# Means of v copied by engines instead of transfers, and a new order of the opening, in an attention and gated-MLP kernel

## The chip, the cores and the metric

One core of one Trainium2 chip. The metric is the device time of one execution in microseconds (us); the median of three runs is 638.13 us (636.65 to 638.30).

## The reference

```python
# q, k, v: (4, 8, 768, 64); w_in: (512, 2048); w_out: (2048, 512)
k_sum = k.reshape(B, H, 24, 32, D).max(axis=3)
v_sum = v.reshape(B, H, 24, 32, D).mean(axis=3)
scores_l = scale * q @ k^T            # kept where |i - j| < 16
scores_s = scale * q @ k_sum^T + log(32)
a = softmax(concatenate([scores_l masked, scores_s]))
attn = a @ concatenate([v, v_sum])
x = attn as (3072 tokens, 512)
h = x @ w_in
out = (h * cos(h)) @ w_out
```

Each query sees 31 neighbours and 24 summaries of its head: block maxima of k, block means of v.

## The kernel before

The 3072 tokens are eight blocks of 384 (two for each batch entry). A block has four attention groups, `a` to `d`, of two heads each (`Group`, so `c1` is the third pair of heads of block 1). Then come steps (`Step`, `s0` to `s127`), one for a block and a slice of 128 of the 2048 hidden columns: 12 `up` products (L728, or in four chunks L740), the gate on ScalarE and VectorE, and 9 `down` products (L788). Products are made of a high and a low part of each operand. Steps `s0` to `s5` are block 0 with slices 0 to 5, `s6` to `s21` are block 1 with all 16 slices, `s22` to `s31` are block 0 with the rest.

A weight slice (`Slice`, `w0` to `w15`) is loaded by SP (L391, L395; 1 MB), taken apart by ScalarE (`ab` L403, `sh` L409), joined by VectorE (`fb` L416) and split into a high part (`hi`, L370 on ScalarE or L372 on VectorE) and a low part (`lo`, L376 on VectorE or GpSimd).

An attention group of the first two blocks goes: loads of q, k, v by SP (L454, L475, L483); transposes on PE (`tk`, `tq`) and copies (`ck`, `cq`, `ks`); mask and score products (`ms` L556, `sc` L581) into two PSUM banks; minimum (`mx` L599, VectorE); six exponentials (`ex` L616, ScalarE); reciprocal (`iv`); `normalize` (`nm` L632, GpSimd); transposes of the probabilities (`tp` L641) and copies (`cp`); `values` (`va` L685, PE) into one bank; high and low part of x (`xh`, `xl`). For `values`, the tile `vn` of a group has 120 partitions: 96 rows of v, loaded by `v`, and 24 block means, brought by `m` (`load_vs`).

The means of batch entry 0 come from 24 products over v (`vm`, L911), read out of PSUM by ScalarE (`ve`, two copies) to `all_means`, a part of the tile `early`. For the eight groups of blocks 0 and 1, `load_vs` then brings 128 columns of them to each of six rows of `vn`, on partitions 96 to 119. For later batch entries it loads from other summaries (`v1_0` and on: `l` loads, `s` sums).

The order of everything is written by hand in `ORDER`, one word for each operation (`group.operation.arguments`; the last letter is the engine: `a` ScalarE, `v` VectorE, `p` GpSimd; digits are PSUM banks or rooms). Every engine and every issuing queue works off its own part of it in that order, and each of them waits in place when an instruction isn't ready. `h0` to `h7` are products of the identity with itself that nothing reads.

Of the kernel before, what the change touches and what calls it, by code (L numbers as in the profile page):

```python
# [1038 lines left out]
```

## Time and profile before

| | |
|---|---|
| median of 3 runs | 638.13 us (636.65 to 638.30) |
| span of the profiled execution | 636.0 us |
| PE busy | 621.8 us (98%) |
| VectorE (DVE) busy | 419.0 us (66%) |
| ScalarE (ACT) busy | 323.8 us (51%) |
| GpSimd (POOL) busy | 195.1 us (31%) |
| DMA queue of SP (q1) | 72.62 MB |
| DMA queue of ScalarE (q10) | 0.72 MB |

The span reaches from the first to the last instruction of one profiled execution; the time of a run is about 2 us longer at the median. Busy shares are means over stages with different limits: what an edit in one stage is worth is read from that stage. In the chain and in the waits, "X <- Y" says that X waited for Y, as far as the semaphore events show; where Y had long been done, it was something else, often a transfer. SPq and ACTq are the queues from which SP and ScalarE issue transfers.

### The profile page before, as it was taken

How to read it: one execution, taken by the hardware profiler on the slowest of the kernel's cores; microseconds unless marked ns; L12 is line 12 of the kernel's file. 1: busy time of each engine (PE TensorE's matmuls, PEld its weight loads, DVE VectorE, ACT ScalarE, POOL GpSimd, SP SyncE). 2: the span in 40 equal slices, each digit the busy share in tenths (PEclk: the TensorE clock that was granted, in tenths of full speed). 3: DMA queues.
4: the chain of work that ended last, by engine and by line, in shares of the span. 5: the costliest groups of instructions: out<-in, count | busy, mean ns of one | idle time of the engine just before them, and what ended most of it. 6: DMA issues, size and time to landing. Idle time of an engine off the chain costs nothing.

```text
span 636.0 us, 12130 instructions
## 1 busy us (share of the span) xinstructions
PE 621.8 (98%) x4568; PEld 545.6 (86%) x4568; DVE 419.0 (66%) x814; ACT 323.8 (51%) x606; POOL 195.1 (31%) x210
## 2 busy tenths in 40 slices
...
GB/s 223 264 239 227 313 127 231 177 63 128 95 137 130 120 92 180 99 83 107 101 101 142 112 80 99 123 63 71 111 93 66 117 74 55 112 38 16 1 1 49
DMA packets 171306, 74.11 MB, mean 117 GB/s; under 512 B 136944, under 2 KB 160112, under 8 KB 171248
## 3 DMA queue, kind: packets, MB, share of 16 engines
q1 hardware_dynamic: 169856, 72.62, 45.3%
q10 hardware_dynamic: 1392, 0.72, 0.5%
q8 instruction: 36, 0.59, 0.4%
q14 instruction: 22, 0.18, 0.1%
HBM read 54.43 MB, written 16.52 MB: 112 GB/s over the span
## 4 chain that ended last, share of the span: by engine, by line
PE 90%; DVE 5%; DMA 2%; ACT 2%; ACTq 1%; issue 1%; SPq 0%; POOL 0%; DVEq 0%; POOLq 0%
PE banks L728 40%; PE banks L788 40%; PE banks L685 3%; PE banks L569 3%; DMA early<-in_v_dram 1%; PE banks L932 1%; DVE stage L416 1%; PE banks L740 1%; ACTq L490 1%; PE banks L581 1%; ACT sc L616 1%; DVE w L376 1%; PE banks L911 0%; PE banks L518 0%; DVE first L372 0%
## 5 line engine op out<-in xcount | busy, mean ns | idle before, releaser
L728 PE MATMUL banks<-xh,w 128*128 128x384 f32 x976 | 255.5, 337 | 0.5 <-DVE t L760 0.5
L788 PE MATMUL banks<-w,gh 128*128 128x512 f32 x768 | 196.5, 392 | 0.0
L728 PEld LDWEIGHTS banks<-xh,w 128*128 128x128 f32 x976 | 176.8, 188 | 3.1 <-issue 0.8
L788 PEld LDWEIGHTS banks<-w,gh 128*128 128x128 f32 x768 | 142.6, 188 | 31.1 <-DVE gh L372 1.6
L728 PE MATMUL banks<-xl,w 128*128 128x384 f32 x488 | 163.2, 334 | 0.0
L376 POOL TENSOR_TENSOR gl<-t,gh 128x384 fp32r<-128x384 f32 x63 | 65.9, 1049 | 286.8 <-DVE gh L372 152.2
L748 ACT ACTIVATE t<-banks 128x384 int32<-128x384 f32 x128 | 62.0, 489 | 126.4 <-PE banks L728 59.8
L751 DVE SCALAR_TENSOR_TENSOR t<-t,banks 128x384 f32<-128x384 int32 x128 | 69.2, 547 | 68.7 <-ACT t L748 67.9
L788 PE MATMUL banks<-w,gl 128*128 128x512 f32 x384 | 108.0, 391 | 0.0
L756 ACT ACTIVATE t<-t 128x384 f32<-128x384 f32 x128 | 65.9, 523 | 63.6 <-DVE t L751 63.3
L728 PEld LDWEIGHTS banks<-xl,w 128*128 128x128 f32 x488 | 91.6, 188 | 0.4
L760 DVE TENSOR_TENSOR t<-t,banks 128x384 f32<-128x384 f32 x128 | 69.5, 548 | 33.1 <-ACT t L756 32.1
L788 PEld LDWEIGHTS banks<-w,gl 128*128 128x128 f32 x384 | 71.6, 188 | 15.7 <-POOL gl L376 0.5
L370 ACT CAST gh<-t 128x384 fp32r<-128x384 f32 x66 | 33.6, 513 | 43.3 <-DVE t L760 24.9
L632 POOL TENSOR_TENSOR sc<-sc,r 128x720 f32<-128x720 f32 x28 | 39.0, 1392 | 47.3 <-DVE r L629 41.5
L604 POOL TENSOR_TENSOR sc<-sc,m 128x720 f32<-128x720 f32 x24 | 34.4, 1433 | 49.6 <-DVE m L596 49.6
L376 DVE TENSOR_TENSOR gl<-t,gh 128x384 fp32r<-128x384 f32 x65 | 36.5, 565 | 12.5 <-ACT gh L370 7.6
L372 DVE CAST gh<-t 128x384 fp32r<-128x384 f32 x62 | 23.1, 373 | 18.1 <-PE banks L788 14.9
L588 DVE SCALAR_TENSOR_TENSOR sc<-banks,mask 128x360 f32<-128x360 f32 x48 | 24.5, 524 | 12.6 <-PE banks L569 12.4
L622 DVE TENSOR_REDUCE r<-sc 128x6 f32<-128x726 f32 x24 | 21.6, 902 | 14.1 <-ACT sc L611 14.0
L376 POOL TENSOR_TENSOR w<-stage,w 128x1024 fp32r<-128x1024 f32 x8 | 19.7, 2468 | 33.5 <-DVE w L372 22.2
L611 ACT ACTIVATE sc<-sc 128x720 f32<-128x720 f32 x24 | 19.4, 807 | 19.0 <-POOL sc L604 18.8
(117 smaller groups left out, 611.0 us busy)
## 6 DMA issues: line engine op xcount, KB each, us to landing
...
```

What stands on the lines that cost most here:

```text
L370: eng.copy(out=out, in_=in_)
L372: eng.tensor_copy(out=out, in_=in_)
L376: eng.tensor_tensor(out=lo, in0=src, in1=hi.bitcast(F32), op=ALU.subtract)
L588: nc.vector.scalar_tensor_tensor(out=self.sc.rearrange("p (c h) n -> p c h n", h=2)[:, :, hh, :], in0=self.sp[hh], scalar=SCALE, in1=mask[ ...
L604: nc.gpsimd.tensor_tensor(out=self.sc, in0=self.sc, in1=self.m.unsqueeze(2).broadcast_to([P, U, NK]), op=ALU.subtract)
L632: nc.gpsimd.tensor_tensor(out=self.sc, in0=self.sc, in1=self.r.unsqueeze(2).broadcast_to([P, U, NK]), op=ALU.mult)
L728: nc.tensor.matmul(out=self.h, lhsT=w_of(name, self.f)[:, c * P : (c + 1) * P], rhs=x_of(self.blk, part, c), start=n == 0, stop=n == last,)
L748: nc.scalar.activation(out=self.t.bitcast(I32), in_=self.h, func=AF.Copy, scale=1.0 / TWO_PI, bias=0.25)
L751: nc.vector.scalar_tensor_tensor(out=self.t, in0=self.t.bitcast(I32), scalar=-TWO_PI, in1=self.h, op0=ALU.mult, op1=ALU.add)
L756: nc.scalar.activation(out=self.t, in_=self.t, func=AF.Sin, scale=-1.0, bias=-0.5 * math.pi)
L760: nc.vector.tensor_tensor(out=self.t, in0=self.t, in1=self.h, op=ALU.mult)
L788: nc.tensor.matmul(out=accs[self.run][i], lhsT=g[:, i * P : (i + 1) * P], rhs=w_of(name, self.f), start=self.first and n == 0, stop=self.l ...
```

## The change

`load_vs` gets an engine as its argument. For blocks 0 and 1 the engine copies the means from `all_means` to the 24 partitions of `vn`, where ScalarE issued a transfer from SBUF to SBUF. For that, `all_means` moves from partitions 0 to 23 of `early` to partitions 96 to 119, the ones to which the copies go. In the order, `c1.m` and `a0.m` are given to VectorE, `d1.m` to ScalarE, and `c0.m`, `d0.m`, `b0.m`, `a1.m` and `b1.m` to GpSimd. The first 559 of the 2098 words of `ORDER` stand in a new order, up to `s20.ga` in block 2; from there on the two are the same. They are the same operations; among them 164 have another bank, room or engine. Group b is now the first to be scored (before: a); the loads `v1_0` to `v1_3` stand behind those of most weights; slices 3, 7 and 11 have their high part on ScalarE and 4, 6, 8, 10 and 12 on VectorE (before the other way round); the low parts of slices 6, 9, 12 and 13 move to GpSimd and that of 15 to VectorE; the sums `v1_0.s` and `v1_4.s` move to GpSimd. The diff is cut: of the order only lines that stand for the beginning of both, up to the first steps.

```diff
-h0.w.3 h2.w.0 h4.w.1 a0.k a0.q b0.q a0.tk.1.5 c0.k a0.tk.0.0 a0.ms.7.6 a0.ks.1 d0.k b0.tq.3 a0.ks.0 b0.k a0.tq.4 c0.q
-a0.ck.1.a a0.ck.0.a h7.w.5 b0.cq.a a0.cq.v a0.sc c0.tk.0.0 c0.tk.1.2 b0.tk.0.4 c0.ks.0 c0.ck.0.a a0.mx.0 w1.l.6 h5.w.1
-a1.q c0.tq.0 h1.w.1 d0.q a0.ex.0 c0.ck.1.v b0.ck.0.a d0.tk.0.6 c0.ks.1 a0.iv b0.tk.1.1 b0.ks.0 d0.tk.1.2 c0.ms.3.7
-c0.cq.v b0.ms.5.0 c0.sc v0_0.l d0.ck.1.a d0.ks.1 b0.ck.1.a d0.ks.0 b0.ks.1 d0.ck.0.v b0.sc w1.ab.0 b1.q w1.sh c0.mx.1
-h6.w.2 a1.tq.6 a1.ms.1.4 v0_1.l v1_0.l d0.tq.2 a1.cq.v c0.ex.1 d0.cq.a a1.sc d0.ms.6.2 d0.sc b0.mx.2 c1.q w1.fb a0.nm
-w1.hi.v a0.tp.1.3 b0.ex.2 v0_0.vm.0 d0.mx.0 d0.ex.3 v0_1.vm a0.v a0.cp.1.a w1.lo.p c0.iv a1.mx.1 v0_1.ve.a b0.iv
-b1.tq.5 a0.tp.0.3 b1.cq.v b1.ms.2.6 b1.sc w0.l.7 d0.iv c0.nm b0.nm a0.m d0.m b0.m d1.q v1_0.s.0.v a1.ex.0 h3.w.5
-a0.cp.0.v d1.m b1.mx.2 c0.m c1.tq.3 v1_1.l c0.tp.0.5 d0.nm c0.v a1.iv a1.nm a1.m c0.tp.1.0 a0.va.4 c1.ms.7.1 c1.cq.v
-c0.cp.0.v d1.tq.3 d0.v a0.xh.a c1.sc v1_1.s.p w2.l.6 b0.v d1.cq.v a0.xl w0.ab.1 b0.tp.1.3 b0.tp.0.5 c0.cp.1.v w0.sh
-d0.tp.0.4 c0.va.0 b1.ex.1 d0.tp.1.6 v1_2.l c1.mx.0 w5.l.1 w0.fb w0.hi.v a1.v w0.lo.p d0.cp.0.a c1.ex.2 b1.iv d0.cp.1.v
-c1.m d1.ms.4.2 c0.xh.v d1.sc c0.xl d0.va.0 b1.nm d1.mx.1 b0.cp.0.a b0.cp.1.v a1.tp.0.7 w2.ab.1 c1.iv a1.tp.1.6 c1.nm
-s1.u.0.3 w2.sh d0.xh.v d1.ex.3 d0.xl b0.va.1 b0.xh.v s0.u.0.5 b0.xl v1_2.s.p s0.u.2 s1.u.2 s1.u.3 a1.cp.0.v c1.tp.1.7
-s1.u.1 s0.u.3 w2.fb w2.hi.v a1.cp.1.a d1.iv d1.v c1.v c1.tp.0.2 s0.u.1 s1.tu.0 w4.l.6 w5.ab.0 a1.va.4 s0.tu.1 w2.lo.v
-w5.sh v1_3.l s0.re d1.nm s1.re s2.u.0.6 s2.u.2 s2.u.3 c1.cp.0.a d1.tp.1.1 c1.cp.1.v c1.va.2 d1.tp.0.0 w3.l.7 s0.si
-w5.fb w5.hi.v d1.cp.1.a b1.tp.0.7 w5.lo.v s1.si s1.ga s0.ga d1.cp.0.a b1.v s2.u.1 d1.va.1 b1.tp.1.0 s5.u.0.5 a1.xh.a
-c1.xh.a w8.l.0 a1.xl s1.hi.0.a s0.hi.1.a d1.xh.v d1.xl s1.lo.0.v s0.lo.1.v w4.ab.1 b1.cp.1.a w4.sh v1_3.s.v s5.u.2
-s2.tu.0 s5.u.3 s2.re b1.m v1_4.l s5.u.1 w4.fb s0.dh.1.0.3 s2.si s0.dl s2.ga s2.hi.1.v s2.lo.1.p w3.ab.0 b1.cp.0.v
-c1.xl w4.hi.a s1.dh s1.dl s2.dh s2.dl w4.lo.v b1.va.4 w3.sh s4.u.0.6 s4.u.2 w9.l.1 b1.xh.a w3.fb w3.hi.v b1.xl s4.u.3
-w3.lo.p s4.u.1 w8.ab.1 s5.tu.1 w7.l.7 s6.up.4 v1_4.s.0.v s4.tu.0 s4.re w8.sh v1_5.l s4.si s5.re s3.u.0.2 s5.si w9.ab.0
...
+h0.w.3 h2.w.0 h4.w.1 b0.k b0.tk.0.0 b0.q h3.w.2 a0.q a0.tq.7 b0.tk.1.4 b0.ck.0.v b0.ck.1.a a0.k b0.ks.0 a0.tk.0.5
+a0.cq.a a0.ck.0.a b0.ks.1 b0.ms.6.3 c0.k c0.q a0.ks.0 b0.tq.2 d0.q b0.cq.v a0.tk.1.0 a0.ck.1.v a0.ks.1 a0.ms.1.4 d0.k
+b0.sc h6.w.7 d0.tq.5 b0.mx.2 c0.tq.2 w1.l.6 d0.cq.v b0.ex.2 v0_1.l a0.sc a0.mx.0 c0.cq.a d0.tk.0.0 d0.tk.1.7 h1.w.6
+d0.ks.1 c0.tk.0.6 d0.ck.0.v d0.ck.1.a a1.q d0.ms.3.5 c0.ck.0.v h5.w.2 b0.iv c1.q a0.ex.0 d0.ks.0 c0.tk.1.7 v0_0.l
+w1.ab.1 w0.l.7 c0.ks.1 c0.ck.1.v w1.sh a0.v c0.v b1.q c0.ks.0 d0.sc d0.mx.1 h7.w.0 a0.iv c0.ms.2.0 w1.fb w2.l.6 a0.nm
+d1.q d0.v b0.v c0.sc d0.ex.3 a1.tq.6 c1.tq.7 a0.tp.0.3 c0.mx.2 a1.cq.a a1.ms.4.6 w1.hi.v c0.ex.1 a0.tp.1.1 a0.cp.0.v
+a1.sc a1.mx.2 d0.iv w1.lo.p v0_0.vm.2 v0_1.vm a1.ex.0 c0.iv w5.l.1 b0.nm v0_1.ve.a c1.cq.v a0.cp.1.v c1.m.v c1.ms.7.3
+a0.m.v c0.nm c0.m.p d0.nm c1.sc w0.ab.1 c0.tp.0.1 w0.sh a1.iv a0.va.0 c0.tp.1.2 a0.xh.a a1.v c1.mx.0 c0.cp.0.v
+c0.cp.1.v c1.ex.2 b0.tp.0.5 c0.va.4 b1.tq.7 a0.xl c0.xh.v w0.fb d0.tp.0.0 b1.ms.1.3 b1.cq.a d0.tp.1.6 d0.m.p c1.iv
+b1.sc w0.hi.v d1.tq.7 a1.nm d0.cp.0.a c0.xl d0.cp.1.a w2.ab.0 c1.v b1.mx.0 d1.ms.0.4 w2.sh d1.cq.v b0.tp.1.2 d0.va.6
+b0.m.p b0.cp.1.v w2.fb w4.l.6 d1.sc b0.cp.0.a d0.xh.v d1.mx.2 w3.l.7 a1.tp.1.2 w0.lo.p s1.u.0.7 d1.v b1.ex.1 s1.u.2
+b0.va.5 s0.u.0.1 d0.xl d1.ex.3 b0.xh.v w5.ab.1 c1.nm w2.hi.v a1.m.p s1.u.3 b0.xl v1_0.l c1.tp.0.6 s0.u.2 w5.sh w2.lo.v
+s0.u.3 b1.v w8.l.0 a1.cp.1.a a1.tp.0.5 s2.u.0.4 s0.u.1 d1.iv s1.u.1 c1.tp.1.3 s0.tu.0 a1.cp.0.v w5.fb s0.re s0.si
+s2.u.2 s1.tu.1 a1.va.5 c1.cp.1.a w5.hi.v d1.nm c1.cp.0.a w5.lo.v s2.u.3 a1.xh.a s0.ga b1.iv s0.hi.1.a a1.xl s1.re
+d1.tp.1.0 s2.u.1 d1.tp.0.2 d1.m.a s0.lo.0.v s5.u.0.3 w9.l.1 s1.si b1.nm s5.u.2 s1.ga s5.u.3 s2.tu.0 s2.re s0.dh.6.5.1
+s2.si s0.dl s1.hi.0.v s2.ga c1.va.7 w4.ab.0 s1.dh s1.lo.1.p b1.tp.0.4 s5.u.1 c1.xh.v d1.cp.0.v s2.hi.1.v w4.sh s1.dl
+c1.xl w4.fb d1.cp.1.a s2.dh w4.hi.v s2.lo.0.p b1.m.p s5.tu.0 w3.ab.1 d1.va.7 v1_0.s.0.p w4.lo.v s4.u.0.2 b1.cp.0.v
+w3.sh s5.re s4.u.2 s5.si s4.u.3 b1.tp.1.0 v1_1.l d1.xh.v s4.u.1 w3.fb s2.dl s4.tu.1 s5.ga s5.hi.0.v b1.cp.1.a w3.hi.a
+b1.va.4 b1.xh.v w3.lo.p s4.re s5.dh b1.xl s4.si v1_1.s.p s5.lo.0.v w8.ab.1 w7.l.7 d1.xl s6.up.0 v1_2.l s3.u.0.7 s4.ga
+s4.hi.0.a s3.u.2 w8.sh s3.u.3 s3.u.1 s11.up.3 s4.lo.1.v s6.tu.1 s3.tu.0 s6.re w8.fb s6.si s3.re w8.hi.v s6.ga w9.ab.0
+s3.si s10.up.2 w8.lo.p s3.ga w9.sh s4.dl w9.fb v1_2.s.p s3.hi.1.a s4.dh s3.dh s3.lo.1.v s3.dl s11.tu.0 w10.l.2 s11.re
+s5.dl w7.ab.1 s11.si w7.sh w9.hi.a s6.hi.1.v s5.ta.1.v s11.ga s6.lo.1.p s10.tu.1 s5.ta.2.v w7.fb v1_3.l s14.up.4
...
@@ -485,11 +484,9 @@
-        def load_vs(self):
+        def load_vs(self, eng=None):
             if not self.b:
-                nc.scalar.dma_start(
-                    out=self.vn[W:NK], in_=means[self.pr].unsqueeze(1).broadcast_to([NB, U, P])
-                )
+                copy(eng, self.vn[W:NK], means[self.pr].unsqueeze(1).broadcast_to([NB, U, P]))
                 return
...
@@ -871,7 +868,7 @@
-    all_means = carve(early, 1280, NB, H * D)
+    all_means = early[W:NK, 1280 : 1280 + H * D]
     means = [all_means[:, i * P : (i + 1) * P] for i in range(NG)]
```

## Rows read from the trace of the kernel before

**Rows 1.** The profile's page: span and instructions of the profiled execution

```profile
span 636.0 us, 12130 instructions
```

**Rows 2.** Stretches: busy us (instructions) of five engines, PE clock, DMA share, GB/s

```profile
0.00:69.00 69.00, 59.73 (x779) 44.75 (x780) 50.34 (x120) 46.31 (x140) 30.63 (x56) 0.98 0.99 244
32.00:40.00 8.00, 6.68 (x113) 5.93 (x114) 5.91 (x13) 6.54 (x24) 3.75 (x6) 0.79 0.85 228
69.00:620.00 551.00, 550.48 (x3739) 491.60 (x3740) 361.91 (x681) 273.00 (x458) 162.45 (x153) 1.00 0.41 103
```

**Rows 3.** PE's waits over the run: total us, times, longest

```profile
PE banks L685 <- ACT pt L370: 2.7, 2, 2.4
PE banks L685 <- ACT sc L616: 2.1, 1, 2.1
PE banks L685 <- DVE w L372: 1.9, 1, 1.9
```

**Rows 4.** Chain that ended last, 26 to 34 us: start, us, what

```profile
27.51 1.04 ACTq L490
...
29.48 1.26 ACTq L490
```

**Rows 5.** Timeline around 45 us: start, us, engine, line, [idle before <- releaser]

```profile
44.70 0.79 ACTq L490 DMA_DIRECT2D late<-early  x1
...
45.61 0.59 ACT L370 COPY pt<-banks 120x512 f32<-120x512 f32 x1 [3.47 <-DMA early<-in_v_dram]
...
46.25 0.92 PE L685 MATMUL banks<-pt,early 120*64 120x64 f32 x24 [2.35 <-ACT pt L370]
```

**Rows 6.** Timeline, 60 to 70 us; packets of q10, 64:66 and 66:69

```profile
60.22 0.79 ACTq L490 DMA_DIRECT2D late<-early  x1
...
q10 hardware_dynamic: 113, 0.05, 11.5%
...
q10 hardware_dynamic: 43, 0.02, 3.3%
...
69.01 0.92 PE L685 MATMUL banks<-pt,late 120*64 120x64 f32 x24 [1.87 <-DVE w L372]
```

**Rows 7.** Timeline of PE, 27 to 38 us: scores, transposes

```profile
27.85 1.09 PE L581 MATMUL banks<-kd,late 64*64 64x96 f32 x48
...
30.16 0.82 PE L641 MATMUL banks<-ident,late 128*120 128x128 f32 x6
...
34.67 1.81 PE L581 MATMUL banks<-kd,qd 64*64 64x96 f32 x48
...
36.41 1.53 PE L641 MATMUL banks<-ident,sc 128*120 128x128 f32 x6
```

**Rows 8.** All DMA queues over the first 40 us

```profile
DMA packets 21578, 9.62 MB, mean 240 GB/s; under 512 B 16568, under 2 KB 21009, under 8 KB 21571
```

**Rows 9.** Groups by line to 165 us: busy us, mean ns, idle before

```profile
L372 DVE CAST w<-stage 128x1024 fp32r<-128x1024 f32 x7 | 4.8, 689 | 0.2
...
L370 ACT COPY first<-kd 128x576 f32<-128x576 f32 x4 | 2.7, 670 | 2.8 <-PE banks L569 2.8
...
L987 POOL MEMSET mask<- 128x384 f32 x1 | 0.4, 418 | 0.0
...
L376 POOL TENSOR_TENSOR w<-stage,w 128x1024 fp32r<-128x1024 f32 x8 | 19.7, 2468 | 33.5 <-DVE w L372 22.2 <-ACT w L370 10.0 <-DMA late<-in_moe_w_out_dram 1.3
...
L632 POOL TENSOR_TENSOR sc<-sc,r 128x720 f32<-128x720 f32 x6 | 8.4, 1393 | 7.8 <-DVE r L629 4.4 <-DMA x<-in_v_dram 3.4
...
L599 DVE TENSOR_REDUCE m<-banks 128x3 f32<-128x360 f32 x16 | 7.7, 524 | 0.5 <-PE banks L581 0.4
...
L372 DVE COPY pt<-banks 120x512 f32<-120x512 f32 x4 | 2.7, 684 | 0.1
```

**Rows 10.** Timeline, 51 to 54 us: GpSimd beside VectorE

```profile
51.04 1.18 DVE L376 TENSOR_TENSOR w<-stage,w 128x1024 fp32r<-128x1024 f32 x1
...
51.27 2.21 POOL L632 TENSOR_TENSOR late<-late,r 128x720 f32<-128x720 f32 x1 [2.65 <-DVE r L629]
```

More of the change, by code (lines that the diff above doesn't have):

```diff
@@ new lines @@
+s7.up.3 s5.st.1 s10.re w7.hi.a w9.lo.p s5.ta.0.a s11.hi.0.a v1_3.s.v s11.lo.0.p s10.si s6.dh.5.7.6 w10.ab.0 w6.l.6
+s6.dl v1_4.l w10.sh s10.ga s5.st.2 w7.lo.v s15.up.2 s8.up.1 s10.hi.1.a v1_4.s.0.p s10.dh a2.q w10.fb s10.lo.1.v w6.ab.1
+v1_5.l s7.tu.0 s8.tu.1 s7.re s7.si w6.sh w10.hi.v s11.dh s8.re v1_5.s.v s7.ga s8.si w6.fb w10.lo.p s7.hi.1.a s10.dl
+s7.lo.1.v s8.ga s15.tu.0 w12.l.7 s8.hi.0.v w12.ab.0 v1_6.l w13.l.6 s15.re w6.hi.v s11.dl s7.dh s8.lo.0.p w12.sh w6.lo.p
+s15.si v1_6.s.v v1_7.l w12.fb s16.up.3 s15.ga w13.ab.1 w12.hi.v s15.hi.1.v w13.sh s16.tu.1 s8.dl s15.lo.0.p w13.fb
@@ new lines @@
+s9.tu.0 w15.lo.v s19.tu.1 s13.dh w14.ab.0 s19.re b2.ks.0 s19.si s9.re w14.sh w11.lo.p s18.dh s18.dl s21.up.0 s19.ga
+w14.fb s9.si c2.kt.1 b2.q s19.hi.1.a s17.up.4 c2.kt.0 s19.lo.1.p a2.kw.a s9.ga s17.tu.1 s13.dl c2.ks.0 a2.sc.3.2 s17.re
+s19.dh w14.hi.a s9.hi.0.v s17.si a2.z.1 s19.dl b2.kw.v s17.ga s9.dh b2.qt d2.k s9.lo.1.v c2.ks.1 a2.z.0 b2.sc.4.1
+w14.lo.p a2.mx.0 s17.hi.1.v s20.up.3 b2.z.0 s23.up.2 s21.tu.0 b2.z.1 a2.su d2.kt.1 s26.up.1 s21.re s17.lo.0.v a2.ex.0
+s20.tu.1 b2.mx.0 b2.su c2.kw.a s17.dh s20.re s20.si a2.sm c2.q s21.si d2.kt.0 c2.qt a2.iv s21.ga a2.nm a2.pt.0 v2_0.l
@@ L66 @@
+c2.sc.0.4 s17.dl d2.q v2_0.s.1.p s20.ga a2.po b2.ex.1 v2_1.l b2.sm c2.z.0 s21.hi.1.a s20.hi.0.a s20.lo.0.v s23.tu.1
 b2.iv s23.re s9.dl s21.dh c2.z.1 a2.pi d2.qt s23.si s20.dl d2.ks.1 s21.lo.1.p s20.dh s21.dl d2.ks.0 s21.ta.2.0.a b2.nm
@@ new lines @@
+b3.sc.2.1 d2.pi d2.va.0 d2.xh.v d2.xl s32.up.6 s32.tu.1 s32.re s32.si s32.ga s32.hi.0.a v2_5.l v2_5.s.p s31.fe.1.0
+s31.ad.1 s33.up.0 s36.up.7 s34.up.4 s33.tu.0 s33.re b3.z.0 s32.lo.1.v s33.si s33.ga s33.hi.1.v a3.ex.0 s34.tu.1
+s31.fe.2.1 s31.ad.2 s38.up.0 b3.z.1 b3.mx.1 v2_6.l s31.st.1 s34.re a3.sm c3.kw.a s35.up.1 s34.si s34.ga s32.dh.2.4.5
+s34.hi.0.a s32.dl s33.dh s33.lo.0.p s33.dl s34.dh c3.q s31.fe.0.0 s31.ad.0 v2_6.s.p a3.v v2_7.l s34.lo.1.p s34.dl c3.qt
+s35.tu.0 s35.re s35.si s35.ga s36.tu.1 s35.hi.1.v s35.lo.0.p s35.dh s35.dl s36.re s36.si c3.sc.1.3 s31.st.0 d3.q
```

222 lines of the change are left out of this document (101 added, 121 removed).

## The prediction

> **What bounds the kernel now.** I read the page first, then busy time by stretches, then PE's waits, and last the instructions around each wait. The span is 636.0 us [rows 1] and TensorE (PE) is busy for 98% of it, so only time in which PE stands still can be won. The stretches say where that is: PE is busy for 59.73 of the first 69 us and for 550.48 of the next 551 [rows 2]. What it idles in the last 16 us is not touched: the new order meets the old one again at `s20.ga` in block 2, with the same PE work behind it. So the sum is made in the first 69 us, where PE idles for 9.3 us. What is saved there moves the end one to one, as long as the full stretch behind it stays full.
>
> PE's waits over the whole run name three of about 2 us, all at the `values` products (L685) [rows 3]; what else they name is at the very start. I went to each of the three.
>
> The first ends at 33.08 us. The chain runs from the products over v (L911) through ScalarE's copies of the means into three DMA issues of L490 (the first and the third here 1.04 and 1.26 us) [rows 4], and then through a1's six exponentials to PE. ScalarE issues those transfers itself, and the exponentials stand behind the first three in its queue; a0's `values` need the PSUM bank that they read.
>
> The second ends at 46.25 us. ScalarE, done with c1's exponentials, stands in front of the issue `c1.m` until 44.70, when the load of b0's v lands; the copy of b0's probabilities waits behind it and starts at 45.61, after 3.47 us of idle time, and PE after that, 2.35 us late [rows 5]. Nothing in that copy needs the load: the wait is the issue's own.
>
> The third ends at 69.01. The profile names a VectorE cast, which belongs to a weight slice and not to `b1.va`. What `b1.va` does need is its means: their transfer was issued at 60.22, the DMA view has no packet of ScalarE's queue from there to 64 us, and 113 and then 43 packets moved from 64 to 66 and from 66 to 69 [rows 6]. A transfer of 72 KB takes about 8 us here, because it shares the DMA engines with the weights. So all three waits belong to the eight transfers.
>
> **Part 1, the transfers go.** Removed from PE: 2.10 + 2.35 + 1.87 = 6.3 us. After the first wait the granted clock is 0.79 on average from 32 to 40 us (part of it at 1.2 GHz, the rest at 2.4), against 1.00 behind 69 us [rows 2], and the same work takes longer: a group of score products 1.81 against 1.09 us, six transposes 1.53 against 0.82 [rows 7]. That is 1.4 us, which goes with the wait that came before it. Together 7.7 us. ScalarE also gets back eight issues of 0.79 us or more [rows 4 to 6], at least 6.3 us, and the DMA engines 0.58 MB (8 x 72 KB), beside the 9.62 MB that they move in the first 40 us [rows 8]. I count neither again.
>
> **Part 2, the copies that replace them.** Each copies 24 partitions of 768 numbers. No row shows this copy; the nearest are VectorE's cast of 1024 numbers, 0.69 us, and ScalarE's copy of 576, 0.67 [rows 9]. By length that is 0.52 us on VectorE (two) and 0.9 on ScalarE (one). For GpSimd (five) the ends are its memset of 384, 0.42 us, doubled to 0.84, and its subtraction of 1024, 2.47, cut to 1.85 [rows 9]; I take 1.2, nearer the first, since a copy has one input. Two stand on PE's path: `c1.m` and `a0.m` on VectorE ahead of a0's `values`, behind ScalarE's two copies of the means. PE has c1's masks and scores and c0's first transposes meanwhile, about 2.1 us, so 0.4 us is left. The five on GpSimd stand between `normalize` operations of 1.39 us [rows 9], and the queue is far from full (30.6 of 69 us [rows 2]). At 1.85 each, b0's would come 2 us later and still before its `values`, since the probabilities are copied later yet; they cost nothing, and at most 1 us without that cover.
>
> One row speaks against using GpSimd: its `normalize` took 2.21 us instead of 1.39 while VectorE ran a weight subtraction beside it [rows 9, 10]. The Trainium skill (SBUF — State Buffer, section "Who interferes with whom") says that the two share a port pair, and that a VectorE instruction with two SBUF inputs contends with a GpSimd instruction that reads SBUF. The trace agrees with that 0.8 us. By this rule one such collision in front of `c0.va` would make the sum 0.8 us smaller.
>
> For the third wait, the Trainium skill (DMA: Bandwidth & Descriptors, section "Anatomy of one DMA — SWDGE (gpsimd) path") gives a fixed cost of about 2.0 us for a transfer, on another issue path. By it b1's means would have been there at about 62.5 us, the third wait would not be theirs, and the sum would be 1.9 us smaller. The packets of rows 6 speak against this, and I leave the sum as it is.
>
> **Part 3, the new order.** It touches 559 steps of 2098, the same ones before and after, so PE's work is the same. I added up durations of this trace along the new text, queue by queue. ScalarE is lighter by about 13 us over the stretch (issues, and casts given to VectorE and GpSimd), VectorE almost equal, GpSimd heavier by about 19. At the first `down` products VectorE has some 42 us of work behind it and ScalarE 40, against PE's 49; before it was 46 and 51 against 52. So ScalarE no longer runs level with PE. New small waits, each followed to its producer: b0's scores now come first, behind one more pair of identity products, 0.5 us; the products over v write bank 2, which c0's exponentials still read, 0.5; the means above, 0.4; `c0.va` behind c1's minima (2 x 0.52) and two copies (0.68 and a shorter one) on VectorE [rows 9], 0.9; the first chunks of slices 2 and 4 behind their low parts (1.18 [rows 10]), 0.4 + 0.3; `b1.va` behind its ScalarE copy, 0.3. The sum is 3.3 us. Bounds: 1 us, if only half of the means, the bank and `c0.va` remain, and 6 us, if each is nearly twice as long.
>
> Loads move on SP's queue. Four loads of v summaries (`v1_0` to `v1_3`) move behind the weights of the first steps, and `w0` and `w2` move ahead of most of v. DMA is nearly full up to 30 us either way. By bytes in issue order (9.6 MB in 40 us), b0's v is complete at about 37 to 41 us and its `values` stand at about 42; b1's v comes at about 57 against 64. I count nothing; without that cover it is 1 to 2 us, which is in the bounds. Farther on, the load of slice 6 moves behind a store of partial sums (`s5.st.1`), to about 83 us by my count, some 10 us later than it was. Its first use is at about 106 us, and landing and conversion take some 16 us. I put it at nothing; it is the first rival.
>
> **The sum.** 7.7 - 3.3 = 4.4 us, with bounds 7.7 - 6 = 1.7 and 7.7 - 1 = 6.7. Span: 636.0 - 4.4 = 631.6 us. The median of the runs, 638.1, is 2.1 above the profiled span, and I carry that: 633.7 us.
>
> **Rivals.** (A) The gain comes, and is partly given back between 90 and 140 us, because slices 6, 12, 13, 15, 11 and 14 arrive later against a PE that is earlier. For it: each load waits for a free place, and a store now stands among them. Against: by my count 5 us of slack at each. At 2.5 us given back the time is 636.2. (B) The change does not do what it says: the waits were really for arriving data, and PE waits as long for the loads of v and weights instead. For it: DMA is at 0.99 of its time in the first 69 us [rows 2]. Against: the second wait ended within 1 us of an issue that needs no v for the copy behind it. Time 637.5 to 638.5. (C) Slower: VectorE's queue stands still at `c1.m.v` until the means are there, and the minima of c1, b1 and d1, copies and weight joins all stand behind it. The two loads of v that feed the means now have `w1` and four loads of q among or ahead of them. I expect the second at about 26 us and the means at 31; every microsecond after that is PE's. To lose 1.9 us the means must be some 6 to 7 us late, which wants loading at about two thirds of the present rate. Against: the same bytes stood ahead of them before (5.3 MB in both orders). At 9 us late the time is 638.1 - 4.4 + 9 = 642.7.
>
> **How the numbers follow.** The forecast has 0.66, A 0.14, B 0.10, C 0.10. A measurement tells about 0.3% (1.9 us) from no change. Faster by more: nearly all of the forecast and a third of A, 0.71. Same: the rest of A, B, and a little of both neighbours, 0.18. Slower: C and its like, 0.11. The forecast's own range is 638.1 - 6.7 to 638.1 - 1.7, or 631.4 to 636.4. I widen it down to 630.8, since the idle time leaves a little more, and up to 637.3 for A and the near side of B; about 0.2 is left out.
>
> **What would show it.** Right: no DMA issues on ScalarE before the steps; PE idle below 6 us in the first 65; no wait of over 1 us at L685; clock 1.00 from 28 to 40 us; b1's `values` near 64 us; PE full from there to 620. Wrong: a wait at L685 or L740 that a v load or a weight ends (B), gaps between 90 and 140 us (A), VectorE idle until the ScalarE copies of L370 into `early` end well after 31 us (C).

## The result, and the profile after

The change makes the kernel slower: 643.2 us at the median (642.15 to 644.1) against 638.2 (636.65 to 639.27) for the kernel before beside it, a ratio of 1.008 [1.006, 1.011]. Forecast were 633.7 us, between 630.8 and 637.3. The page of the kernel after:

```profile
span 641.9 us, 12137 instructions
PE 624.2 (97%) x4568; PEld 544.9 (85%) x4568; DVE 435.3 (68%) x819; ACT 319.7 (50%) x596; POOL 217.5 (34%) x227
```

VectorE is busy 16 us longer than before (419.0), with five instructions more. Its stretches (columns as in [rows 2]):

```profile
0.00:69.00 69.00, 62.18 (x819) 46.69 (x820) 56.90 (x124) 48.06 (x141) 37.64 (x57) 1.00 0.95 233
32.00:40.00 8.00, 6.36 (x127) 5.43 (x129) 7.59 (x17) 6.38 (x19) 7.10 (x5) 1.00 0.91 227
...
69.00:90.00 21.00, 20.51 (x106) 18.30 (x104) 18.12 (x25) 16.08 (x23) 14.31 (x13) 1.00 0.53 183
90.00:115.00 25.00, 20.87 (x93) 18.14 (x94) 20.89 (x26) 13.68 (x18) 12.85 (x9) 0.93 0.62 189
115.00:165.00 50.00, 48.55 (x303) 42.49 (x302) 44.99 (x80) 32.27 (x50) 21.07 (x17) 1.00 0.57 129
165.00:620.00 455.00, 454.51 (x3173) 404.54 (x3172) 284.39 (x548) 203.16 (x353) 129.60 (x132) 1.00 0.37 92
```

The opening did gain: TensorE is busy for 62.18 us of the first 69 instead of 59.73, at the full clock where before it fell to 0.79 [rows 2]. b1's `values` start at 67.23 us instead of 69.01 [rows 6], without the wait, and 12 more `up` products of 0.17 us stand ahead of them: 1.78 + 2.1 = 3.9 us. Then it is lost. Before, PE was full from 69 us on [rows 2]; now it idles for 4.1 us between 90 and 115, with the clock at 0.93 there, and for 1.5 us between 115 and 165. From 3.9 us ahead to a span 6.0 us longer (5.98 before rounding), the kernel loses 9.9 us behind 67 us.

```profile
67.23 0.92 PE L682 MATMUL banks<-pt,late 120*64 120x64 f32 x24
```

PE's waits over the run (total, times, longest), the first in place of those of [rows 3]:

```profile
PE banks L725 <- DVE t L757: 2.7, 3, 1.9
PE banks L785 <- ACT gh L369: 2.1, 1, 2.1
PE banks L929 <- POOL ident masks.py:199: 1.4, 1, 1.4
PE banks L502 <- DMA qn<-in_q_dram: 1.0, 1, 1.0
```

The wait of 2.1 us is at 100.8 us, behind a VectorE that stood 2.3 us for a load of v; the one of 1.9 us is at 108.5. What VectorE and GpSimd do around them (start, us, what; L260, L269 and L271 belong to the sums of v, L375 on GpSimd is a low part of weights, L757 is the multiplication of the gate for which PE waits):

```profile
98.03 1.04 DVE L260 TENSOR_REDUCE part_sum<-kn 96x64 f32<-96x512 f32 x1 [2.33 <-DMA kn<-in_v_dram]
...
100.80 1.65 PE L785 MATMUL banks<-w,gh 128*128 128x512 f32 x6 [2.09 <-ACT gh L369]
...
102.75 1.02 POOL L375 TENSOR_TENSOR gl<-t,gh 128x384 fp32r<-128x384 f32 x1 [5.17 <-DVE gh L371]
102.99 1.33 DVE L371 CAST w<-stage 128x1024 fp32r<-128x1024 f32 x1
...
104.40 2.40 POOL L375 TENSOR_TENSOR w<-stage,w 128x1024 fp32r<-128x1024 f32 x1 [0.63 <-DVE w L371]
...
105.37 1.51 DVE L269 TENSOR_TENSOR vs<-vs,part_sum 96x64 f32<-96x64 f32 x1
106.81 1.21 DVE L415 SCALAR_TENSOR_TENSOR stage<-late,first 128x1024 int32<-128x1024 int32 x1
107.94 0.54 DVE L757 TENSOR_TENSOR t<-t,banks 128x384 f32<-128x384 f32 x1
...
108.53 0.45 PE L725 MATMUL banks<-xh,w 128*128 128x384 f32 x1 [1.89 <-DVE t L757]
...
110.49 5.72 POOL L375 TENSOR_TENSOR w<-stage,w 128x1024 fp32r<-128x1024 f32 x2
...
112.65 1.29 DVE L269 TENSOR_TENSOR vs<-vs,part_sum 96x64 f32<-96x64 f32 x1
113.97 2.28 DVE L271 TENSOR_SCALAR vs<-vs 96x64 f32<-96x64 f32 x1
```

An addition of 64 columns takes 1.51 us, and ends 0.1 us behind GpSimd's subtraction (106.80). The cast ahead of it, 0.69 us in the kernel before [rows 9], takes 1.33. At 112.65 and 113.97 two such small instructions end one after the other with GpSimd's next two. In the kernel before they take 0.22 and 0.19 us. The groups to 165 us show it as means (busy us, mean ns), first the kernel before, then after:

```profile
L416 DVE SCALAR_TENSOR_TENSOR stage<-late,first 128x1024 int32<-128x1024 int32 x16 | 19.5, 1219 | 2.1 <-ACT first L409 1.2 <-POOL gl L376 0.7
L376 DVE TENSOR_TENSOR xl<-banks,xh 128x384 fp32r<-128x384 f32 x8 | 4.4, 554 | 1.7 <-ACT xh L370 1.6
L270 DVE TENSOR_TENSOR vs<-vs,part_sum 96x64 f32<-96x64 f32 x4 | 0.9, 222 | 0.2
L272 DVE TENSOR_SCALAR vs<-vs 96x64 f32<-96x64 f32 x2 | 0.4, 192 | 0.1
```

```profile
L415 DVE SCALAR_TENSOR_TENSOR stage<-late,first 128x1024 int32<-128x1024 int32 x16 | 24.6, 1537 | 2.3 <-ACT first L408 1.3 <-issue 0.9
L375 DVE TENSOR_TENSOR xl<-banks,xh 128x384 fp32r<-128x384 f32 x8 | 4.4, 548 | 0.0
L269 DVE TENSOR_TENSOR vs<-vs,part_sum 96x64 f32<-96x64 f32 x4 | 3.7, 926 | 0.3
L271 DVE TENSOR_SCALAR vs<-vs 96x64 f32<-96x64 f32 x2 | 3.2, 1602 | 0.1
```

I call it a **stop** when a VectorE instruction, up to 170 us, takes over 0.25 us more than the median of its line and shape in the kernel before (the copies of the means, which that kernel lacks, are left out). The kernel before has none. The kernel after has 22, 17.5 us in all; each began while a GpSimd instruction was running, and ended, to within 0.25 us, its own usual time behind that one's end. An instruction with an operand in PSUM (`xl` above) is never stopped, nor is a reduction, a transpose or a reciprocal. Of the others between 12 and 170 us, one of 63 begins beside a running GpSimd instruction in the kernel before (0.2 us before its end), and 28 of 66 in the kernel after.

### The profile page after: what moved, and what is told of

Read it like the earlier page. It is cut to its first block, busy times and chain, and to the rows that moved or that the text cites. A ratio compares the mean times of both kernels' runs of the same rounds, so it can differ in the third digit from the quotient of the medians.

```text
span 641.9 us, 12137 instructions
## 1 busy us (share of the span) xinstructions
PE 624.2 (97%) x4568; PEld 544.9 (85%) x4568; DVE 435.3 (68%) x819; ACT 319.7 (50%) x596; POOL 217.5 (34%) x227
## 4 chain that ended last, share of the span: by engine, by line
PE 77%; DVE 9%; DMA 7%; ACT 3%; SPq 2%; issue 2%; POOL 1%; DVEq 0%; POOLq 0%; ACTq 0%
PE banks L785 35%; PE banks L725 34%; DMA late<-in_moe_w_out_dram 3%; PE banks L682 3%; PE banks L566 3%; DVE stage L415 2%; DMA kn<-in_v_dram 1%; PE banks L929 1%; ACT first L408 1%; DVE gl L375 1%; ACT stage L402 1%; DMA x<-in_v_dram 1%; SPq L453 1%; DMA late<-in_v_dram 1%; PE banks L737 1%
## 5 line engine op out<-in xcount | busy, mean ns | idle before, releaser
L375 POOL TENSOR_TENSOR gl<-t,gh 128x384 fp32r<-128x384 f32 x66 | 67.4, 1023 | 273.8 <-DVE gh L371 150.4
L785 PE MATMUL banks<-w,gl 128*128 128x512 f32 x384 | 109.4, 395 | 0.3 <-DVE gl L375 0.3
L757 DVE TENSOR_TENSOR t<-t,banks 128x384 f32<-128x384 f32 x128 | 69.5, 546 | 32.6 <-ACT t L753 31.6
L369 ACT CAST gh<-t 128x384 fp32r<-128x384 f32 x60 | 30.6, 511 | 42.9 <-DVE t L757 25.2
L375 DVE TENSOR_TENSOR gl<-t,gh 128x384 fp32r<-128x384 f32 x62 | 37.5, 607 | 12.0 <-ACT gh L369 7.0
L371 DVE CAST gh<-t 128x384 fp32r<-128x384 f32 x68 | 25.7, 379 | 18.0 <-PE banks L785 14.1
L375 POOL TENSOR_TENSOR w<-stage,w 128x1024 fp32r<-128x1024 f32 x11 | 28.5, 2596 | 15.0 <-DVE w L371 7.7
```

The source lines that it names most:

```text
L369: eng.copy(out=out, in_=in_)
L371: eng.tensor_copy(out=out, in_=in_)
L375: eng.tensor_tensor(out=lo, in0=src, in1=hi.bitcast(F32), op=ALU.subtract)
L757: nc.vector.tensor_tensor(out=self.t, in0=self.t, in1=self.h, op=ALU.mult)
L785: nc.tensor.matmul(out=accs[self.run][i], lhsT=g[:, i * P : (i + 1) * P], rhs=w_of(name, self.f), start=self.first and n == 0, stop=self.l ...
```

## The experiments

Two theories at first. **Queue**: the loads v1_0 to v1_7 of v share one buffer, so each waits for the sum before it; moved late, they hold up weights on SP's queue and the engines that stand in front of them. **Stops** (called ports or collisions in the expectations): VectorE loses its time behind GpSimd. All ratios are to the kernel before on the same chip.

| run | ratio [95%] | median, us | stops, us in all |
|---|---|---|---|
| after | 1.0082 [1.0060, 1.0105] | 643.2 | 22, 17.5 |
| e1 copies alone, old order | 0.9994 [0.9976, 1.0013] | 636.8 | 2, 2.7 |
| e2 new order alone, transfers | 1.0367 [1.0335, 1.0399] | 660.0 | 17, 14.8 |
| e3 after, sums of v as before | 1.0167 [1.0134, 1.0200] | 646.8 | 15, 14.4 |
| e4 after, low parts as before | 1.0110 [1.0083, 1.0137] | 643.7 | 12, 9.3 |
| e5 old order, ScalarE's copies | 0.9946 [0.9927, 0.9965] | 635.2 | 0 |
| e6 after, sums on GpSimd | 1.0116 [1.0091, 1.0141] | 645.6 | 18, 13.7 |
| e7 after, short low parts | 1.0012 [0.9992, 1.0032] | 639.0 | 17, 9.8 |
| e8 = e6 + e7 | 1.0046 [1.0028, 1.0064] | 641.3 | 17, 10.1 |
| e9 after, one sum later | 1.0079 [1.0056, 1.0101] | 642.5 | 20, 16.3 |
| e10 = e7 + e9 | 1.0002 [0.9981, 1.0023] | 637.7 | 17, 9.9 |
| e11 after, ScalarE's copies | 1.0118 [1.0089, 1.0148] | 646.0 | 18, 15.4 |
| e12 e5, slice 0 later | 1.0009 [0.9991, 1.0027] | 638.3 | 1, 2.2 |
| e13 = e10 + short gates | 0.9985 [0.9965, 1.0005] | 637.2 | 14, 8.2 |
| e14 = e5 + seven new engines | 0.9940 [0.9921, 0.9959] | 634.5 | 4, 4.1 |
| e15 e5, slice 0 later, again | 1.0011 [0.9998, 1.0024] | 639.0 | 0 |
| e16 after, weights ahead | 1.0154 [1.0114, 1.0194] | 649.5 | 18, 11.9 |
| e17 = e10 + weights ahead | 1.0091 [1.0056, 1.0126] | 645.4 | 15, 8.6 |
| e18 = e10 + second buffer | 0.9981 [0.9961, 1.0001] | 636.9 | 17, 9.8 |

### Copies alone, order alone (e1, e2)

e1 puts the copies, with the engines of the change, into the old order; e2 puts the new order on the transfers.

```diff
-a0.m d0.m b0.m ... d1.m ... c0.m ... a1.m ... c1.m ... b1.m
+a0.m.v d0.m.p b0.m.p ... d1.m.a ... c0.m.p ... a1.m.p ... c1.m.v ... b1.m.p
```

> The kernel before with the copies in place of the eight transfers (same engines for them as in the changed kernel), its order kept word for word otherwise. Queue theory (the loss comes from where the loads of the v summaries stand in the new order): the order is the old one, so nothing is lost and the three waits of rows 3 go, 5 to 7 us: 631 to 633 us. Port theory (the loss comes from GpSimd and VectorE hindering each other): the copies bring a part of that, 2 to 4 us are lost again: 634 to 637 us. If the copies themselves were what made the changed kernel slower: above 640 us.

> The new order with the eight transfers put back (issued by ScalarE where the new order has the copies). Queue theory: the loss behind 68 us stays and the waits for the transfers come on top, 645 to 650 us. Port theory: five GpSimd and two VectorE copies fewer, so VectorE is busy 5 us less up to 165 us, and the time is near that of the changed kernel or below it, 640 to 644 us.

The copies alone change nothing, the order alone costs 3.7%. In e2 ScalarE's queue stands for a load of v until 37.5 us, then issues transfers, and a0's `values` start at 45.4 us after 14.8 us of idle time: this order needs the copies. But with 17 stops, 14.8 us, it has nearly as many as the kernel after, and no copy of means on VectorE or GpSimd. So most of the stops come with the new order and its engines, and not with the copies.

### ScalarE's copies in the old order, and one pair of instructions (e5)

```diff
-a0.m.v d0.m.p b0.m.p ... d1.m.a ... c0.m.p ... a1.m.p ... c1.m.v ... b1.m.p
+a0.m.a d0.m.a b0.m.a ... d1.m.a ... c0.m.a ... a1.m.a ... c1.m.a ... b1.m.a
```

> The order of before, with all eight means copied by ScalarE (none by VectorE or GpSimd). With the means split over the engines this order took 636.8 us. There a copy of VectorE took 2.13 us behind GpSimd's weight subtraction and a subtraction of VectorE 2.78 us at 121 us. Collision theory (VectorE and GpSimd stop one another, and these stops ate the gain): the stops are gone, ScalarE's copies cost 8 x 0.83 us where it issued eight transfers, the gain of the opening comes, 631 to 634 us. Rival (the arrival of the weights sets the pace between 115 and 165 us, whatever the opening gains): 636 to 638 us.

The time lies 1.2 us above the one range and 0.8 below the other; e5 has no stop at all, and beats both kernels. In the kernel before, e1 and e5 PE has the same instructions in the same order, so their starts can be compared one by one. At b1's `values` e1 is 1.3 us ahead of the kernel before and e5 2.8; behind 126 us e1 is 0.2 us ahead. So e1 loses 1.4 us against e5 in the opening and about 1.1 at one pair, VectorE's low part of a gate (`gl`) and GpSimd's low part of a weight, both free when the same cast ends. The kernel before, e5, and e1 with the PE instruction that came of it:

```profile
122.88 0.55 DVE L376 TENSOR_TENSOR gl<-t,gh 128x384 fp32r<-128x384 f32 x1
123.04 2.67 POOL L376 TENSOR_TENSOR w<-stage,w 128x1024 fp32r<-128x1024 f32 x1 [9.62 <-DVE w L372]
```

```profile
120.01 0.55 DVE L377 TENSOR_TENSOR gl<-t,gh 128x384 fp32r<-128x384 f32 x1
120.17 2.65 POOL L377 TENSOR_TENSOR w<-stage,w 128x1024 fp32r<-128x1024 f32 x1 [9.56 <-DVE w L373]
```

```profile
121.43 2.40 POOL L377 TENSOR_TENSOR w<-stage,w 128x1024 fp32r<-128x1024 f32 x1 [9.49 <-DVE w L373]
121.46 2.78 DVE L377 TENSOR_TENSOR gl<-t,gh 128x384 fp32r<-128x384 f32 x1
...
125.82 0.96 PE L787 MATMUL banks<-w,gh 128*128 128x512 f32 x3 [0.56 <-ACT gh L371]
```

VectorE 0.16 us earlier: GpSimd pays 0.3 us. GpSimd 0.03 us earlier: VectorE pays 2.23 us, and PE waits. In e1's opening `c1.m`, a copy on VectorE behind another weight subtraction, took 2.13 us, and PE waited 2.3 us at 42.4 (for a low part on VectorE). e5's stretches from 69 us on are full:

```profile
0.00:69.00 69.00, 62.02 (x814) 47.77 (x815) 51.39 (x122) 54.56 (x151) 31.30 (x56) 0.95 0.98 240
69.00:90.00 21.00, 21.00 (x114) 19.90 (x113) 17.79 (x28) 17.91 (x25) 8.99 (x5) 1.00 0.74 234
90.00:115.00 25.00, 25.00 (x128) 22.58 (x127) 21.45 (x35) 19.69 (x30) 4.30 (x4) 1.00 0.84 208
115.00:165.00 50.00, 50.00 (x349) 43.99 (x348) 38.23 (x73) 32.49 (x54) 22.11 (x19) 1.00 0.42 102
```

### Parts of the new order put back (e3, e4, e11)

e3 puts the loads and sums of v back to where they stood and to their old engines; e4 gives five low parts their old engines; e11 gives the new order ScalarE's copies.

```diff
-w6.lo.p w9.lo.p w12.lo.p w13.lo.p w15.lo.v
+w6.lo.v w9.lo.v w12.lo.v w13.lo.v w15.lo.p
```

> The changed kernel with the loads and sums of the eight v summaries (v1_0 to v1_7) put back beside the neighbours, and on the engines, that they had in the order before; all other words stay. Queue theory: SP is no longer held by them between 60 and 112 us, the weights come some 10 us earlier, and most of the 9.6 us lost behind 68 us comes back: 633 to 637 us. Port theory: GpSimd loses only two sums, 640 to 643 us.

> The changed kernel with the low parts of weight slices 6, 9, 12, 13 (to VectorE) and 15 (to GpSimd) on the engines that they had before; the order stays. Port theory: three subtractions of 2.6 us fewer on GpSimd, VectorE's instructions beside them get shorter (its join of 1.54 us on average back toward 1.22) by more than the 4 x 1.2 us that it takes over, and the time falls by 2 to 4 us: 639 to 641 us. Queue theory: VectorE has more work in the stretch in which it is late already, 643 to 646 us.

> The kernel after with all eight means copied by ScalarE, as the faster run did in the order of before (there 1.6 us faster than with the split copies). Collision theory: of the 16.6 us of stops some 2.5 us stand next to a copy; little of that is on the path, since most of the loss comes behind 85 us: 641.5 to 643.5 us. If the copies were the cause, as in the order of before: 640 to 641.5 us.

e3 is slower than either theory had it: PE's waits in its opening are 2.6 us for a copy of means that stands behind the sums on GpSimd (42 us) and 1.6 us for q, and at 113 us PE still waits 2.7 us for a gate on VectorE. e4 halves the stops, but VectorE gets four subtractions of 1.22 us for one that it gives up, and nothing is won, against the forecast of the stop theory: fewer stops are worth something only if VectorE isn't paid for them. e11 shows that ScalarE's copies are no gain by themselves: in the new order PE waits 2.2 us at 36 us and 3.0 at 103 us, and it is slower.

### Shorter operations on GpSimd (e7, e10, e13)

e7 halves GpSimd's low parts of weights (the other half is left out of the computation); the `down` products keep their number, shapes and waits. e10 is e7 with the later sum of e9 below. e13 also cuts GpSimd's low parts of gates to a third.

```diff
-            rest(eng, wm[self.f][:, 2 * DM :], self.uf, wm[self.f][:, : 2 * DM])
+            n = DM if eng is nc.gpsimd else 2 * DM
+            rest(eng, wm[self.f][:, 2 * DM : 2 * DM + n], self.uf[:, :n], wm[self.f][:, :n])
```

> The kernel after; GpSimd's low parts of the weight slices take 512 of 1024 columns, and the down products that would read the other half read the first half (the low part of w_out of eleven slices is left out of the computation). TensorE's work and what it waits for are as before. Collision theory: VectorE stands for about half as long behind these eleven operations, and the wait of 1.9 us at 108 us goes with the half clock behind it: 637.5 to 640.5 us. Queue theory: the loads of v and weights are as late as they were, 642 to 643.5 us.

> The later sum together with GpSimd's shorter low parts (again the low part of w_out of eleven slices is left out). With the short low parts alone 639.0 us. If stops and stand are two causes on the path, the wait of 1.6 us that was left at 99 us goes: 636.5 to 638 us. If they are one: 639 us.

> As the run with the later sum and the short low parts (637.7 us), and GpSimd's low parts of the gates of the steps s0 to s21 take 128 of 384 columns (the rest, and the low part of w_out of eleven slices, is left out; the products are as many and wait for the same instructions). Ten stops of VectorE were left next to those, of 0.3 to 0.9 us. If stops are the rest of the loss: 635 to 636.5 us. If it is the order itself (short waits at the steps from 133 to 165 us): 637 to 638.5 us.

e7 gives 0.7% (about 4.5 us) back, the largest single step, and no stop is longer than 1.2 us. At the gate behind the addition of above PE waits 0.8 us instead of 1.9:

```profile
105.50 0.45 PE L728 MATMUL banks<-xh,w 128*128 128x384 f32 x1 [0.78 <-DVE t L760]
```

VectorE's own work is the same; but GpSimd is also ready 1.1 us sooner each time, so the edit does not weigh the stops alone. (None of PE's waits between 69 and 165 us in the kernel after names GpSimd, though.) PE's instructions and their order are the same in both, so it can be told where the two profiles part: e7 is 1.3 us ahead at 72 us, 1.9 behind the wait at 101, 3.0 behind the gate at 108.5 and 4.5 at 113, where the kernel after has run at 1.2 GHz and e7 at 2.4. The further steps of e10 and e13 lie within the intervals.

### Seven of the new engines in the old order (e14)

```diff
-w6.lo.v w9.lo.v w12.lo.v w13.lo.v w15.lo.p v1_0.s.0.v v1_4.s.0.v
+w6.lo.p w9.lo.p w12.lo.p w13.lo.p w15.lo.v v1_0.s.0.p v1_4.s.0.p
```

> The order of before with ScalarE's copies (635.2 us, no VectorE instruction stopped), and the engines of the kernel after for seven operations: the low parts of slices 6, 9, 12 and 13 and the sums v1_0 and v1_4 to GpSimd, the low part of slice 15 to VectorE. VectorE gets some 6 us less to do, GpSimd some 12 us more. If stops come with the work on GpSimd: VectorE instructions are stopped for some 4 us or more, and the time is 636.5 to 640 us. If they come with the new order's timing: few stops, 634 to 636 us.

Four stops of 4.1 us come with the work, all between 70 and 111 us, and the time is the best of all runs, level with e5. PE idles for 0.2 us from 69 to 115 and not at all from there to 165; 3.7 us ahead of the kernel before at b1's `values`, it is still 2.9 ahead at the end. So these stops cost 0.8 us at most, and more work on GpSimd isn't by itself the cause. A stop costs time where an instruction that PE needs stands behind it and VectorE has no idle time in between, as ahead of 108.5 us in the kernel after; that the four of e14 fall into such idle time is my reading, not shown. Besides the copies, 53 operations have another engine in the new order. The 46 that e14 leaves alone, among them the high parts of eight slices, are tested by no run apart from the order.

### Standing in front of loads of v (e6, e8, e9, e16 to e18)

e6 gives VectorE's four sums of v to GpSimd; e9 moves one sum six words later; e16 moves loads of weights ahead of those of v on SP's queue; e18 gives every other load of v a second buffer.

```diff
-s8.re v1_5.s.v s7.ga s8.si w6.fb w10.lo.p
+s8.re s7.ga s8.si w6.fb v1_5.s.v w10.lo.p
```

```diff
-w3.fb ... v1_1.l ... w7.l.7 v1_2.l ... w10.l.2 ... v1_3.l ... w6.l.6 v1_4.l
+w3.fb w7.l.7 w6.l.6 v1_1.l ... w10.l.2 v1_2.l ... v1_3.l ... w12.l.7 v1_4.l
```

> The kernel after, with the four sums of v that VectorE has (v1_3, v1_5, v1_6, v1_7) given to GpSimd. Queue theory (VectorE stands at the landing of a load of v, 2.3 us at 96 us, and TensorE waits 2.1 us for what is behind it and then runs at the half clock for 3.4 us): 638.5 to 640.5 us. Collision theory (the time goes because VectorE is stopped while GpSimd reads SBUF): five of the stopped instructions are these sums' own (5.9 us of 16.6), but GpSimd gets 7 us more to do, 640.5 to 643.5 us.

> Both edits of the two runs before this one. If the two causes lie in a row on the path, their gains add up: 635 to 638 us. If they are one and the same cause, no more than the better of the two alone: 638 to 640.5 us. If neither is the cause: 642 to 644 us.

> The kernel after; one word, VectorE's sum of v1_5, stands six words later, behind the gate of slice 7 and the join of slice 6. In the kernel after VectorE stands 2.3 us in front of it until a load lands, and a TensorE wait of 2.1 us hangs on the gate behind it; given to GpSimd it held a low part for 4.8 us. Queue theory (an engine that works in order stands at the load, whoever it is): that wait goes, 640 to 641.5 us, and 1 to 2 us better yet if the half clock behind 109 us goes too. Collision theory alone (the stand only moves time that the stops take anyway): 642 to 643.5 us.

> The kernel after (643.2 us); on SP's queue the loads of slices 7, 6, 10, 12, 13 and 15 stand ahead of the loads v1_1 to v1_7 that they stood behind, as early as their room allows; nothing else moves. If late weights are a cause beside the stops (ScalarE stood 0.7 and 1.9 us for them at 92 and 107 us): 639.5 to 641.5 us. If not: 642 to 644 us, or worse, since the sums of v on VectorE and GpSimd then wait longer for their loads.

> The same loads ahead, with the later sum and GpSimd's short low parts (637.7 us without the loads; the low part of w_out of eleven slices is left out). If stops and late weights are the whole loss, the opening's 5 us come through: 632 to 635 us. If something else sets the pace behind 100 us: 636.5 to 639 us.

> The order of the kernel after with the later sum and GpSimd's short low parts (637.7 us; the low part of w_out of eleven slices is left out), and a second buffer for the loads v1_1, v1_3, v1_5 and v1_7 (part of a key tile that is free from 50 to 130 us). A load then no longer waits for the sum just before it, and a sum finds its load landed. If stops and this chain are the whole loss, the 5 us of the opening come through: 632.5 to 635 us. If something else sets the pace behind 100 us: 636.5 to 638.5 us.

In e6 GpSimd stands in front of the load of v1_5, and a low part behind it is late (GpSimd's and PE's rows):

```profile
97.71 1.74 POOL L251 TENSOR_TENSOR kn<-kn 96x256 f32<-96x256 f32 x2 [3.18 <-DMA kn<-in_v_dram]
...
100.19 2.33 POOL L376 TENSOR_TENSOR w<-stage,w 128x1024 fp32r<-128x1024 f32 x1
...
102.58 1.01 PE L726 MATMUL banks<-xh,w 128*128 128x384 f32 x2 [4.77 <-POOL w L376]
```

e9 takes the wait of 2.1 us at 101 us down to 0.5, and the median stays: the wait at the next gate, 2.4 us at 106 us, takes its place. e16 and e17 show what late loads of v cost: 0.7 and 0.9% more than the same kernels without the move. In e16 VectorE stands in front of them for 8.8 us (waits of VectorE from 60 to 165 us), and PE waits 4.1 us at 114 us for a gate on VectorE:

```profile
DVE part_sum L261 <- DMA kn<-in_v_dram: 8.8, 4, 3.5
```

With a second buffer (e18) these stands are gone, and the gain over e10 is 0.2%, within the intervals. So the place of the loads of v is worth several microseconds when it gets worse, but their chain is not what is left.

### Two attempts to go further (e12, e15)

e5 still has a wait of 2.4 us at 39.3 us, for b1's exponentials behind ScalarE's work on slice 0, and runs at 0.95 of the clock in the first 69 us.

```diff
-w0.ab.1 ... w0.sh ... b1.ex.1 ... w0.fb w0.hi.v ... d0.cp.0.a c1.ex.2 ... b0.cp.0.a
+b1.ex.1 ... d0.cp.0.a b0.cp.0.a w0.ab.1 w0.sh c1.ex.2 ... w0.fb w0.hi.v
```

In e15 c1's exponentials go ahead, too (and d1's; c1's copy of the means and the work on slice 2 move back):

```diff
-d0.cp.0.a b0.cp.0.a w0.ab.1 w0.sh c1.ex.2 ... w0.fb w0.hi.v ... w0.lo.p
+d0.cp.0.a b0.cp.0.a c1.ex.2 w0.ab.1 w0.sh ... w0.fb w0.hi.v w0.lo.v
```

> The order of before with ScalarE's copies (635.2 us), and one group of words moved: b1's exponentials, and the copies of d0's and b0's probabilities, stand ahead of ScalarE's work on slice 0, and the first products of slice 0 behind those of slice 1. There TensorE waited 2.4 us at 39.3 us for b1's exponentials and ran at the half clock from 38.9 to 45.7 us. If that wait is the last one in its place: 631 to 633 us. If slice 0, now some 3 us later, or another wait takes its place: 634 to 637 us.

> A second attempt at the wait of 2.4 us at 39.3 us in the order of before with ScalarE's copies: b1's exponentials, d0's and b0's copies and c1's exponentials stand ahead of ScalarE's work on slice 0 (the attempt before left c1's behind it, and TensorE waited 4.2 us for the bank that they read), slice 0's low part is VectorE's, and its products stand behind those of slice 1. If the opening's gain is passed on: 631.5 to 634 us. If slice 0 or a stop of VectorE takes it back: 635 to 637.5 us.

Both moved the wait. PE's waits from 20 to 70 us, the first of e12, then two of e15:

```profile
PE banks L639 <- ACT late L614: 4.2, 1, 4.2
```

```profile
PE banks L738 <- DVE w L372: 2.7, 2, 1.4
PE banks L639 <- ACT late L614: 1.9, 1, 1.9
```

In e12 the transposes need a bank that c1's exponentials still read; in e15 slice 0 is late, and 1.9 us of that wait are left. No gain of the opening was made, so they don't tell whether a larger one would be passed on.

## Why the prediction was wrong

**Opening, parts 1 and 3.** Forecast was a gain of 4.4 us there; it was 3.9. No wait of more than 1 us is left at `values` (L682), the clock is 1.00 from 32 to 40 us, and PE idles for 6.8 us of 69 (I had put it below 6 of 65). With the three waits gone, that leaves new waits of 3.9 us, where I had 3.3. That this total is so near is in part luck: a wait of 1.0 us for a load of q at 38.6 and one of 0.8 for a `normalize` on GpSimd at 30.8 were not in my list, and those for bank 2 (0.5) and `c0.va` (0.9) did not come. b1's `values` came at 67.2 us, not near 64, with 2.1 us more of `up` products ahead of them. So the sum held, in this order. Part 1 by itself bought less: in the old order, without the transfers, PE is 2.8 us ahead at b1's `values` in e5 and 1.3 in e1, where I had 7.7. In e5 the second and the third wait are gone and 1.1 us of the first is left, but a wait of 2.4 us at 39.3 has come, and 6.8 us at 1.2 GHz instead of 3.4.

**"What is saved there moves the end one to one, as long as the full stretch behind it stays full."** This is the step that failed. I took the full stretch for granted, and examined behind 69 us only the loads of weights. PE's idle time from 90 to 165 us went from 0 to 5.6 us, and the clock fell to 1.2 GHz for 3.4 us behind the waits of 2.1 and 1.9 us: 0.93 over 25 us is 1.75 us of work. Together with 0.5 us from 69 to 90 these rows hold 7.8 of the 9.9 us lost; the rest I can't assign. The clock's part is that of the profiled execution: of the four behind the median one ran at 1.000 throughout, and took 642.15 us, more than any of the kernel before beside it.

**VectorE beside GpSimd, part 2.** The one pair I had found [rows 10] I counted as a loss of GpSimd, 0.8 us off the sum at most. It is the largest term that I can place: 22 stops, 17.5 us of VectorE. I had read the row one way round (VectorE first, GpSimd waits); the other way round was not in the trace of before, which has no stop, and its price is up to 2.1 us here. The Trainium skill (SBUF — State Buffer, section "Who interferes with whom") has more than the rule that I took from it: copies, casts and `tensor_scalar` operations can hold the shared ports too, and whoever comes first keeps them for the whole instruction while the other fully blocks. The trace agrees: casts, a 64-column `tensor_scalar` (2.28 us) and joins were stopped, and nothing that reads PSUM. I also compared VectorE's load (42 us against PE's 49) as if its durations were fixed.

How much of the 9.9 us are stops? The wait of 1.9 us at 108.5 can be placed: VectorE has no idle time from 99.6 us to the instruction for which PE waits, and two stops lie in it, 0.64 us at the cast at 103.0 and 1.29 at the addition at 105.4, together 1.9; without them the wait would be gone, unless something else took its place. Halving the low parts gives 4.5 us back (e7), with the reservation above; of the profiled gain, 1.1 us came at this gate and 1.5 from the clock behind it. The share of the other stops is argued, not shown. The stops come with this order and its engines (e2; e14 has four of them), which let GpSimd's subtractions start just ahead of VectorE's instructions; in the old order VectorE's begin beside a running GpSimd once.

**Copies, part 2.** I put the five on GpSimd at nothing and the two on VectorE at 0.4 us. Their prices were 0.83 us on ScalarE (0.9 forecast), 1.40 and 1.18 on VectorE (0.52; 0.56 where nothing stops it, in e7), and on GpSimd 0.82 to 1.71 (1.2). Alone they changed nothing (e1): the opening gained less than with ScalarE's copies, and most of that gain went at the pair of e1 above. On ScalarE alone they give 0.5% (e5).

**"I count nothing" for the loads of v, part 3.** Too low, and I had looked at it only for the opening. VectorE stood 2.3 us and GpSimd 3.2 us in front of such loads in the kernel after, and the wait of 2.1 us at 101 us is behind the former; e16 and e17 price later loads at 4.5 to 6 us. That wait alone is not the loss, though (e9).

**Rivals.** A had the place (90 to 140 us) and the reason "weights late", at 2.5 us. Weights are late in the kernel after (ScalarE waits 1.9 us for one at 107 us), but PE's wait behind that hangs on VectorE, and with loads of weights ahead, and those of v behind, it only got slower. C, the side on which the time came out, did not happen: VectorE waited 1.1 us at `c1.m`, not 9.

**What stays open.** e18 is 2 us slower than e5 though its opening is no worse; 17 stops of 9.8 us remain in it, and PE idles for 2.6 us from 69 to 165, where e5 idles not at all. The longest of these waits, 1.3 us at 103.7, is at the same gate; in VectorE's work ahead of it the cast is still stopped for 0.64 us and the addition held for 0.2. Whether the other stops or the order's own short waits up to 135 us make the rest was not separated.
